# One order for all steps of an attention and channel-mix kernel

## The chip, the core and the metric

The kernel runs on one core of a Trainium2 chip. A core has engines that work side by side, each through its own instructions in their order: TensorE multiplies matrices (PE in the profile; PEld are its weight loads), VectorE (DVE) and ScalarE (ACT) work elementwise, SyncE (SP) issues DMAs and calculates nothing. An instruction that needs another engine's result waits on a semaphore, and everything behind it on its engine waits too. The metric is the time of one execution on the device in microseconds (us); lower is better.

## The reference

Attention inside chunks of 64 tokens for 8 batches of 8 heads, 576 tokens, head size 64; then a channel mix over the 512 joined channels, with 1024 hidden ones. q, k and v are float32, the mu vectors and the weights float64 at the input; the kernel computes with pairs of float32 values, a high part and a low part.

```python
q_c, k_c, v_c = (x.reshape(B, H, nc, 64, D) for x in (q, k, v))
scores = (1 / sqrt(D)) * matmul(q_c, k_c.transpose(0, 1, 2, 4, 3))
attn = softmax(scores)                        # over the last axis
x = matmul(attn, v_c).reshape(B, H, S, D)     # heads joined to 512 channels
x_prev = x shifted by one token, 0 at the start of a batch
xk = mu_k * x + (1 - mu_k) * x_prev
xr = mu_r * x + (1 - mu_r) * x_prev
out = sigmoid(xr @ w_r) * (relu(xk @ w_k) ** 2 @ w_v)
```

## The kernel before

The 4608 tokens are worked in 36 tiles t of 128 tokens (two chunks), or 18 groups g of 256. Every piece of work is a step with a name, a small function that issues a few instructions. An order written out by hand, as a text of step names, says in which sequence the steps issue; since each engine is in order, the text fixes the order on every engine and on every DMA queue. A letter behind a name chooses the engine of an elementwise step (`:A` ScalarE, `:D` VectorE) or, for a load, ScalarE's DMA queue instead of SP's. Before, there are two texts, `START` for the first groups and all weights, and `LATER` for the rest; the second begins where the first has ended. The steps that matter here:

- `nk0 nq0` load q and k of the first three groups in their natural layout, `T` moves them through TensorE (even numbers, 16 matmuls each: T0.6 and T0.4 are the two halves of k, T0.0 and T0.2 of q) and out of PSUM (odd numbers). From the fourth group on, `bq`, `bk` load blocks, each word 4 to 8 DMAs, and `D` transposes them on VectorE (D10.0 for q, D10.1 for k of tile 10). `v` loads v of a tile with four DMAs.
- `S` is the softmax of a tile: scores on TensorE (S.0), maximum, subtraction, exp, sum, scaling. Two tiles of a group share one PSUM tile. `P` transposes the result (P.0), copies it (P.1), multiplies by v (P.2) and writes x (P.3, P.4).
- `s`, `c`, `h` load and convert a weight from float64 bits (`swr1` is half of w_r; c.0, c.1 on ScalarE, c.2, c.3 on VectorE, h.0 high half, h.1 low half). `mu` loads (mu.0), transposes (mu.1, TensorE) and copies the two vectors; `dg` makes diagonal matrices of them.
- `Mk`, `Mr` mix x with its predecessor and split the result in two halves. `R` is the product with w_r and its sigmoid, `K` the product with w_k of a group (24 matmuls of 256 columns) with relu, square and two halves, `V` the product with w_v (steps 0 to 7 of three matmuls of 512 columns, then the multiplication by the sigmoid, then the store).
- From group 4 on, two groups together form the w_k product as a 2 x 2 block product with seven multiplications instead of eight (`U` sums of weights, `Xt` and `X` sums of inputs, `M` the products, `C` and `E` the rest). START with K00 to K13 and the K2, K3 of LATER stand before that; I call the stretch from one to the other the passage, and what follows from V30 on the pairs.
- `W:9` issues nine matmuls on an idle tile (two instructions each) that compute nothing.

Scratch tiles are given out in turn: `bank("k")` alternates between two PSUM banks k0, k1, `bank("o")` between o0 and o1, and `mixed` and `f_relu` go round a few SBUF tiles, in the order of the calls.

```python
    with tc.manual_schedule():
        for word in START.split():
            name, _, e = word.partition(":")
            if name == "W":
                for _ in range(int(e)):
                    nc.tensor.matmul(warm, idle, idle, start=True, stop=True)
            else:
                fn, engine_of = first.pop(name)
                fn(e or engine_of)
```

Of the kernel before, what the change touches and what calls it, by code (L numbers as in the profile page):

```python
# [1261 lines left out]
```

## Time and profile before

| | us |
|---|---|
| median of three runs (608.8 to 612.25) | 609.77 |
| the profiled execution, its own time | 608.68 |
| its span, first to last instruction | 606.9 |
| TensorE busy | 586.3 |
| VectorE busy | 469.8 |
| ScalarE busy | 371.9 |

The span is what the trace shows; 1.8 us of the execution's time lie around it. Busy is the time in which an engine had at least one instruction under way. An engine that waits inside a stretch is not busy; matmuls are pipelined, so a busy TensorE isn't one at its peak.

### The profile page before, as it was taken

To read this page: it belongs to the slowest core of one execution; us is meant where nothing else is said; L and a number is where in the kernel's file an instruction comes from. 1 tells how busy PE (TensorE), PEld (TensorE's weight loads), DVE (VectorE), ACT (ScalarE), POOL (GpSimd) and SP (SyncE) were. 2 spreads that over 40 slices of the span, in tenths; PEclk is the share of its full clock that TensorE was granted. 3 is DMA by queue.
4 is the path that set the end of the run, shared out by engine and by line. 5 is a ranking of instruction groups with operands and counts; after the bars stand their busy time and mean duration, and the time that the engine had idled before them with its cause. 6 is when DMAs were issued, how large, how long until landed. Compare 5 with 4: busy or idle time off the path is not lost.

```text
span 606.9 us, 14236 instructions
## 1 busy us (share of the span) xinstructions
PE 586.3 (97%) x5633; PEld 514.4 (85%) x5633; DVE 469.8 (77%) x991; ACT 371.9 (61%) x599; POOL 0.7 (0%) x6
## 2 busy tenths in 40 slices
PE   6799999997999999999999999999999999999997
PEld 6689888986878987898889888888898889888985
DVE  0788898887999797988796988798869886965321
ACT  3599974372755872689267817791579257924640
POOL 0000000000000000000000000000000000000000
PEclk8899999999999999999999999999999999999999
DMA  9698243244324324434432342334324341000001
GB/s 264 162 312 207 36 112 75 34 91 88 69 43 98 55 55 109 75 68 70 92 65 59 67 95 33 89 66 94 55 63 71 89 80 45 13 36 36 1 18 52
DMA packets 186802, 49.19 MB, mean 81 GB/s; under 512 B 172392, under 2 KB 178544, under 8 KB 186736
## 3 DMA queue, kind: packets, MB, share of 16 engines
q1 hardware_dynamic: 179664, 46.45, 33.7%
q10 hardware_dynamic: 7072, 1.84, 1.3%
q8 instruction: 44, 0.72, 0.5%
q14 instruction: 22, 0.18, 0.1%
HBM read 38.80 MB, written 9.44 MB: 79 GB/s over the span
## 4 chain that ended last, share of the span: by engine, by line
PE 73%; SPq 12%; DMA 6%; DVE 4%; ACT 4%; issue 2%; DVEq 0%; ACTq 0%
PE pv L845 26%; PE m L1143 20%; PE pr L811 13%; SPq L359 9%; PE pk L767 4%; PE s L531 3%; PE xps L611 3%; DMA nat<-in_k 2%; SPq L323 2%; PE pt L588 2%; DMA qT<-in_q 1%; PE trk L484 1%; DMA mus<-in_moe_mu_r 1%; DMA v<-in_v 1%; DMA kT<-in_k 1%
## 5 line engine op out<-in xcount | busy, mean ns | idle before, releaser
L845 PE MATMUL pv<-wv,kk 128*128 128x512 f32 x864 | 209.8, 397 | 0.2 <-ACT sg L827 0.2
L845 PEld LDWEIGHTS pv<-wv,kk 128*128 128x128 f32 x864 | 159.4, 188 | 37.6 <-ACT sg L827 0.6
L811 PE MATMUL pr<-wr,xr 128*128 128x512 f32 x432 | 106.1, 397 | 0.0
L811 PEld LDWEIGHTS pr<-wr,xr 128*128 128x128 f32 x432 | 79.5, 188 | 18.1 <-issue 0.2
L1194 DVE TENSOR_TENSOR kk<-c,kk 128x512 fp32r<-128x512 f32 x56 | 38.0, 684 | 29.1 <-ACT kk L276 29.1
L767 PE MATMUL pk<-xk,wk 128*128 128x256 f32 x384 | 48.0, 283 | 0.9 <-ACT relu L781 0.9
L767 PEld LDWEIGHTS pk<-xk,wk 128*128 128x128 f32 x384 | 46.5, 188 | 1.7 <-ACT relu L781 1.1
L1143 PE MATMUL m<-t,wk 128*128 128x256 f32 x336 | 44.9, 283 | 0.0
L1143 PE MATMUL m<-xk,wk 128*128 128x256 f32 x336 | 43.2, 281 | 0.0
L1143 PEld LDWEIGHTS m<-t,wk 128*128 128x128 f32 x336 | 42.1, 188 | 1.0
L1143 PE MATMUL m<-t,sum 128*128 128x256 f32 x336 | 42.3, 282 | 0.1
L1143 PEld LDWEIGHTS m<-xk,wk 128*128 128x128 f32 x336 | 41.7, 188 | 0.6
L1143 PEld LDWEIGHTS m<-t,sum 128*128 128x128 f32 x336 | 40.7, 188 | 0.6 <-DVE sg L858 0.5
L1162 DVE TENSOR_TENSOR c<-m,c 128x512 f32<-128x512 f32 x42 | 28.6, 686 | 14.2 <-PE m L1143 13.5
L858 DVE TENSOR_TENSOR sg<-pv,sg 128x512 f32<-128x512 f32 x36 | 24.7, 686 | 18.5 <-PE pv L845 18.2
L541 DVE TENSOR_REDUCE m<-s 128x8 f32<-128x512 f32 x36 | 23.7, 683 | 18.3 <-PE s L531 18.3
L276 ACT ACTIVATE x<-xps 128x512 f32<-128x512 f32 (+1 forms) x40 | 20.8, 548 | 26.7 <-DMA qT<-in_q 15.4
L1187 ACT ACTIVATE c<-c 128x512 f32<-128x512 f32 x56 | 35.3, 631 | 1.3
L1181 ACT ACTIVATE c<-c 128x512 f32<-128x512 f32 x42 | 26.3, 626 | 15.8 <-DVE c L1162 15.3
L276 ACT ACTIVATE kk<-c 128x512 fp32r<-128x512 f32 x56 | 34.9, 631 | 1.5
L1031 DVE SCALAR_TENSOR_TENSOR mixr<-d,mu,x 128x128 f32<-128x128 f32 (+1 forms) x124 | 33.3, 333 | 0.2
L531 PE MATMUL s<-kT,qT 64*64 64x64 f32 x1152 | 26.7, 227 | 4.5 <-DVE kT L507 2.3
(108 smaller groups left out, 843.4 us busy)
## 6 DMA issues: line engine op xcount, KB each, us to landing
v<-in_v SPq DMA_DIRECT2D x144, 64.0 KB, 2.6
out<-sg SPq DMA_DIRECT2D x36, 256.0 KB, 2.1
wk_st<-in_moe_w_k SPq DMA_DIRECT2D x4, 1024.0 KB, 6.1
wv_st<-in_moe_w_v SPq DMA_DIRECT2D x4, 1024.0 KB, 14.9
qT<-in_q SPq DMA_DIRECT2D x128, 32.0 KB, 1.9
kT<-in_k SPq DMA_DIRECT2D x128, 32.0 KB, 1.9
qT<-in_q SPq DMA_DIRECT2D x48, 24.0 KB, 1.8
wr_st<-in_moe_w_r ACTq DMA_DIRECT2D x1, 1024.0 KB, 6.4
```

Source lines behind the costliest of these rows:

```text
L276: nc.scalar.activation(to, x, AF.Copy)
L359: queue(e).dma_start(out=to_s[:, i], in_=of[:, i])
L531: nc.tensor.matmul(scores()[halves[e], j, hp, :], qT[halves[j], hp, cols[e]], kT[halves[j], hp, cols[e]], start=True, stop=True,)
L767: nc.tensor.matmul(pk[:, e, :], wk[f // 4][:, a, cb, f % 4 * P : (f % 4 + 1) * P], xk[b][:, cb, :], start=(n == 0), stop=(n == 3 * NB - 1),)
L811: nc.tensor.matmul(pr, xr[a][:, cb, tl * TT : (tl + 1) * TT], wr[b][:, cb, :], start=(n == 0), stop=(n == 3 * NB - 1),)
L845: nc.tensor.matmul(T[f"pv{g}{tl}"], kk[a][:, f, tl * TT : (tl + 1) * TT], wv[b, f // 4][:, f % 4, :], start=(f == 0 and n == 0), stop=(f = ...
L1031: nc.vector.scalar_tensor_tensor(out=to[:, s : s + w], in0=d[:, cb, s : s + w], scalar=mu[:, cb : cb + 1], in1=x[:, cb, c : c + w], op0=AL ...
L1143: nc.tensor.matmul(ps[w][:, e, :], left(n, a, cb, 2 * u + e), right(g, n, b, cb), start=first and i == 0, stop=i == 11, skip_group_check=True,
L1162: nc.vector.tensor_tensor(r(i), ps[where[n]], r(i), ALU.add)
L1181: nc.scalar.activation(r(i), x, AF.Relu)
L1187: nc.scalar.activation(r(i), r(i), AF.Square)
L1194: engine[e].tensor_tensor(lo, r(i), f32(hi), ALU.subtract)
```

## The change

The two texts become one, `ORDER`, over all steps, in another sequence throughout. Each scratch tile is now looked up by name in a table (`HOMES`), which says for the first four groups which bank or tile it takes. The loads of `nq`, `nk` and `v` can choose their queue like the others. Beyond that no step is added or taken away except the fillers: `W:9`, `W:4`, `W:4`, `W:3` become one `W:17` at the head. 92 elementwise steps that ran on ScalarE carry `:D` now. The w_r half `swr1` goes to SP's queue, mu.0 stays on ScalarE's and comes first.

```diff
-START = """
-W:9 Mk2.0:D nk0.0 T0.6 nq0.0 T0.4 swr1.0:A T0.7:A P0.3:D T0.5:A T0.0 T0.2 T0.1:A mu.0 nk1.0
-T0.3:A W:4 S0.0 cwr1.0:A mu.1 S1.0 S0.1:D W:4 T1.4 S0.2:D S0.3:A mu.2:A S1.1:D T1.5:A nq1.0 W:3
-T1.2 S1.2:D S1.3:A S0.4:D S0.5:D S1.4:D T1.0 S1.5:D v0.0 P0.0 cwr1.1:A T1.3:A T1.1:A cwr1.2:D
...
-K01.2:A K01.3:A cwv0.3:D K03.1:A K10.0 cwv1.0:A Mk0.0:D K03.2:A swv3.0 K11.0 bk3.0 bk3.1 bk3.2 bk3.3 S5.1:D
-R11.1:A K01.4:D cwv1.2:D cwv1.3:D bq4.0 bq4.1 bq4.2 bq4.3 hwv0.0:A K10.1:A hwv0.1:D K12.0 V001.0 S4.3:A cwv3.1:A
...
-V10.5 bk4.0 bk4.1 bk4.2 bk4.3 Mr4.2:D V10.6 V10.7 D7.1:D D6.0:D V10.8:D V10.9 V11.6 v7.0 V11.7 Mr5.2:D V11.8:D V11.9
-LATER = """
...
-bk5.2 V21.0 Mk7.1:D P9.1:A V21.1 Mr6.1:A Mk6.3:D V21.2 Mk7.2:A bk5.3 V21.3 Mk7.3:D D10.0:D V21.4
-D11.0:D V21.5 Mr6.2:D U61.0:A V21.6 V20.8:D V21.7 Mr7.0:D V20.9 K30.0 Mr7.1:A D10.1:D D11.1:D
...
+ORDER = """
+W:17
+mu.0:A nk0.0 P0.3:D nq0.0 swr1.0 nk1.0 nq1.0 T0.6 T0.4 T0.7:A v0.0 T0.0 T0.5:A T0.2 T0.1:D T0.3:A
+S0.0 nk2.0 S1.0 cwr1.0:A mu.1 S0.1:D swr0.0 cwr1.1:A S1.1:D S0.2:D T1.6 mu.2:A cwr1.2:D T1.4 v1.0
+S0.3:A S1.2:D T1.7:A S0.4:D T1.5:A T1.0 S0.5:D S1.3:A T1.1:A S1.4:D P0.0 T1.2 dg.0:A P0.1:D S1.5:D
+nq2.0 cwr1.3:D P1.0 T2.6 swk1.0 P1.1:D P0.2 T1.3:A hwr1.0:D P0.4:A S2.0 hwr1.1:D v2.0 S3.0
...
+V001.3 S5.3:A hwv3.1:D K11.3:A V001.4 S4.5:D bk4.0 K11.4:D V001.5 S5.4:D S5.5:D V001.6 K10.3:D
+K10.4:D P4.0 D7.0:D K12.1:A bq4.3 V001.7 D7.1:D P4.1:A D6.1:D K12.2:A P5.0 V001.10:D K12.3:A P4.2
+P5.1:A K12.4:D V11.0 P4.4:A V001.8:D K13.0 Mk4.0:D v6.0 Mk4.1:D Mr4.0:D V10.0 Mk4.2:A V10.1
+K13.1:A V001.9 V11.1 K13.2:A P5.3:D V001.11 Mk4.3:D K13.3:A V11.2 bq4.1 D6.0:D Mr4.1:A V10.2
...
+V20.5 V21.7 bk5.2 Mk6.3:D Mk7.2:A V20.6 Mk7.3:D V20.7 Mr7.0:D v9.0 K31.0 Mr6.2:D Mr7.1:A D10.0:D
+D11.0:D V21.8:D K30.0 V11.9 K31.1:A D10.1:D v10.0 K31.2:A D11.1:D Mr7.2:D U61.0:A V20.8:D K31.3:A
+P8.3:D S10.0 P9.3:D K30.1:A U61.1:D P9.2 U51.1:D K30.2:A V10.9 S11.0 P9.4:D K30.3:A v11.0 R30.0
...
+V170.2 V171.3 V171.4 V171.5 V171.6 V170.3 V170.4 V170.5 V170.6 V170.7 V171.7 V170.8:D V171.8:D
+V170.9 V171.9
...
     def bank(tag, shape, name):
-        tag = turn(("k0", "k1")) if tag == "k" else turn(("o0", "o1")) if tag == "o" else tag
+        if tag in ("k", "o"):
+            tag = PLACE[name]
         return ps_m.tile(shape, F32, tag=tag, name=name)
...
-                    nc.sync.dma_start(
+                    queue(e).dma_start(
                         out=dst[s // 2 : (s + n) // 2, :, :, :],
...
-        for word in LATER.split():
+        for word in ORDER.split():
             name, _, e = word.partition(":")
```

The old order ended in `V171.6 V171.7 V171.8:D V171.9`, with V170 stored before.

## Rows read from the trace of the kernel before

**Rows 1.** Busy time on the page: us, share of the span, instructions.

```profile
PE 586.3 (97%) x5633; PEld 514.4 (85%) x5633; DVE 469.8 (77%) x991; ACT 371.9 (61%) x599; POOL 0.7 (0%) x6
```

**Rows 2.** Busy time by stretch: stretch (us), its length, then busy time and instructions of PE, PEld, DVE, ACT, POOL, the granted TensorE clock as a share of 2.4 GHz, the DMA engines' busy share, GB/s.

```profile
21.08:45.00 23.92, 21.56 (x365) 18.88 (x366) 21.31 (x36) 22.47 (x45) 0.00 (x0) 1.00 0.70 238
108.00:170.00 62.00, 57.31 (x646) 50.48 (x645) 51.94 (x110) 35.32 (x56) 0.00 (x0) 1.00 0.34 70
170.00:512.00 342.00, 339.36 (x3341) 298.01 (x3345) 289.97 (x646) 215.70 (x352) 0.00 (x0) 1.00 0.35 71
...
19.26:58.60 39.34, 36.98 (x495) 32.67 (x495) 35.02 (x49) 35.86 (x62) 0.00 (x0) 0.98 0.76 230
58.60:108.40 49.80, 49.80 (x418) 43.44 (x417) 44.37 (x87) 36.23 (x53) 0.00 (x0) 1.00 0.33 73
```

**Rows 3.** What TensorE waited for: waiting line, released by, us in total, times, longest.

```profile
PE trk L484 <- DMA nat<-in_k: 3.2, 1, 3.2
PE mu_t L374 <- DMA mus<-in_moe_mu_r: 3.1, 1, 3.1
PE s L531 <- DVE kT L507: 2.3, 1, 2.3
```

**Rows 4.** The start in order of time: start, length (us), engine, line, operation, out<-in, shape, count.

```profile
1.05 3.67 PE L914 MATMUL warm<-idle 128*128 128x128 f32 x18 [1.05 <-DVE x L628]
...
7.89 3.38 PE L484 MATMUL trk<-ident,nat 128*64 128x128 f32 x32 [3.17 <-DMA nat<-in_k]
...
11.09 2.00 PE L484 MATMUL trq<-ident,nat 128*64 128x128 f32 x32
...
13.03 1.16 PE L914 MATMUL warm<-idle 128*128 128x128 f32 x8
...
14.12 0.69 PE L531 MATMUL s<-kT,qT 64*64 64x64 f32 x32
...
17.90 0.24 PE L374 MATMUL mu_t<-ident,mus 8*128 8x8 f32 x1 [3.08 <-DMA mus<-in_moe_mu_r]
...
18.07 1.13 PE L531 MATMUL s<-kT,qT 64*64 64x64 f32 x32
...
19.26 0.69 DVE L541 TENSOR_REDUCE m<-s 128x8 f32<-128x512 f32 x1 [18.25 <-PE s L531]
```

**Rows 5.** Busy time by stretch, columns as in rows 2, for the first loads (the last column is GB/s): SP's queue alone, then with w_r on ScalarE's, then SP's alone again.

```profile
2.00:3.00 1.00, 1.00 (x7) 1.00 (x6) 0.00 (x0) 0.54 (x1) 0.00 (x0) 1.00 0.49 132
3.00:6.00 3.00, 1.72 (x11) 1.53 (x10) 0.00 (x0) 0.00 (x0) 0.00 (x0) 1.00 1.04 395
6.00:12.00 6.00, 4.11 (x48) 4.04 (x48) 0.00 (x0) 1.27 (x2) 0.00 (x0) 0.72 1.19 297
```

**Rows 6.** Busy time by stretch, columns as in rows 2, cut where the granted clock changes.

```profile
1.05:4.01 2.96, 2.96 (x14) 2.96 (x15) 0.00 (x0) 1.28 (x1) 0.25 (x1) 1.00 0.55 185
4.01:7.42 3.41, 0.71 (x6) 0.52 (x5) 0.00 (x0) 0.00 (x0) 0.00 (x0) 1.00 1.05 362
7.42:10.84 3.42, 2.95 (x28) 2.98 (x30) 0.00 (x0) 0.63 (x1) 0.00 (x0) 0.50 1.22 291
...
17.66:21.08 3.42, 3.18 (x41) 2.90 (x41) 1.78 (x3) 0.36 (x1) 0.00 (x0) 0.50 0.90 151
```

**Rows 7.** SP's queue in order of time from 60 to 156 us, columns as in rows 4; the first and the last of eleven groups of issues that follow one another without a pause, and three between.

```profile
74.59 10.18 SPq L359 DMA_DIRECT2D nat<-in_k  x16
...
101.36 0.85 SPq L862 DMA_DIRECT2D out<-sg  x2
102.31 2.61 SPq L323 DMA_DIRECT2D v<-in_v  x4
104.96 16.56 SPq L359 DMA_DIRECT2D nat<-in_k  x32
...
140.87 8.00 SPq L359 DMA_DIRECT2D nat<-in_k  x16
148.97 6.51 SPq L862 DMA_DIRECT2D out<-sg  x2
```

**Rows 8.** TensorE in order of time, columns as in rows 4, in the passage (P8.0, K30.0, S10.0) and behind it (S16.0, P16.0).

```profile
139.18 1.17 PE L588 MATMUL pt<-ident,p 128*128 128x128 f32 x8 [1.36 <-DVE p L561]
...
145.78 3.00 PE L767 MATMUL pk<-xk,wk 128*128 128x256 f32 x24
...
152.14 1.20 PE L531 MATMUL s<-kT,qT 64*64 64x64 f32 x64 [2.27 <-DVE kT L507]
...
240.85 1.69 PE L531 MATMUL s<-kT,qT 64*64 64x64 f32 x64 [1.33 <-issue]
...
257.85 1.17 PE L588 MATMUL pt<-ident,p 128*128 128x128 f32 x8 [0.35 <-DVE p L561]
```

**Rows 9.** Groups of VectorE's instructions by line and shape: count, busy us, mean ns of one, idle before.

```profile
L1194 DVE TENSOR_TENSOR kk<-c,kk 128x512 fp32r<-128x512 f32 x56 | 38.0, 684 | 29.1 <-ACT kk L276 29.1
...
L278 DVE CAST wr<-wr_st 128x1024 fp32r<-128x1024 f32 x1 | 0.7, 694 | 0.0
```

**Rows 10.** The end in order of time, columns as in rows 4.

```profile
599.64 3.65 PE L845 MATMUL pv<-wv,kk 128*128 128x512 f32 x15
...
603.33 0.69 DVE L858 TENSOR_TENSOR sg<-pv,sg 128x512 f32<-128x512 f32 x1 [4.90 <-PE pv L845]
604.05 0.33 SPq L862 DMA_DIRECT2D out<-sg  x1
```

More of the change, by code (lines that the diff above doesn't have):

```diff
@@ new lines @@
+V41.5 P14.4:A Mk13.0:D V50.0 bk8.3 Mr13.0:D V50.1 V41.6 V41.7 Mk13.1:D bq8.3 Mr13.1:A V50.2 V50.3
+V41.8:D Mk13.2:A V50.4 bq8.1 P15.3:D Mr13.2:D P15.4:A V50.5 D17.1:D V50.6 D16.1:D V51.0 V40.9
+Mk13.3:D V41.9 R60.0 Mk14.0:D v16.0 Mr14.0:D Mk14.1:D V50.7 R60.1:A D16.0:D R61.0 v17.0 V50.8:D
+D17.0:D Mk15.0:D Mk15.1:D V51.1 R61.1:A V50.9 Xt37.0:D Mr14.1:A S16.0 S17.0 X7t3.0:A Mr14.2:D
+V51.2 bq9.0 S16.1:D V51.3 S16.2:D V51.4 S17.1:D S16.3:A V51.5 bk9.0 S16.4:D R70.0 S16.5:D S17.2:D
+bq9.1 X7t3.1:D S17.3:A S17.4:D P16.0 M6a.0 bq9.3 S17.5:D R70.1:A Xt17.0:D M6a.1 C6a.0:A Xt17.1:D
@@ new lines @@
+V170.2 V171.3 V171.4 V171.5 V171.6 V170.3 V170.4 V170.5 V170.6 V170.7 V171.7 V170.8:D V171.8:D
+V170.9 V171.9
+"""
+HOMES = dict(
+    F0="""
+relu_0_0 relu_0_2 relu_1_0 relu_1_2 relu_2_0 relu_2_2 relu_3_0 relu_3_2
+""",
+    F1="""
+relu_0_1 relu_0_3 relu_1_1 relu_1_3 relu_2_1 relu_2_3 relu_3_1 relu_3_3
+""",
+    X0="""
+diag_k0 d_3 mixk_4 mixr_5 d_7
+""",
+    X1="""
+diag_k1 mixk_3 mixr_4 d_6 mixk_7
+""",
+    X4="""
+diag_r0 mixr_3 d_5 mixk_6 mixr_7
+""",
+    X5="""
+diag_r1 d_4 mixk_5 mixr_6
@@ new lines @@
+""",
+    k0="""
+trk1_0 trq0_0 mu_t trk0_1 trq1_1 trk0_2 trq1_2 pk_0_1 pk_0_3 pk_1_1 pk_1_3 pk_2_1 pk_2_3 pk_3_1
+pk_3_3
+""",
+    k1="""
+trk0_0 trq1_0 trk1_1 trq0_1 trk1_2 trq0_2 pk_0_0 pk_0_2 pk_1_0 pk_1_2 pk_2_0 pk_2_2 pk_3_0
+pk_3_2
+""",
+    o0="""
+warm mxr_0 mxr_1 pr_0_1 mxk_2 pr_1_1 pv_0_1 pv_1_1 pr_2_1 pv_2_1 pr_3_1 pv_3_1
+""",
+    o1="""
+mxk_0 mxk_1 pr_0_0 mxr_2 pr_1_0 pv_0_0 pv_1_0 pr_2_0 pv_2_0 pr_3_0 pv_3_0
+""",
+)
+PLACE = {name: tag for tag, names in HOMES.items() for name in names.split()}
@@ L649, in mixed @@
     def mixed(shape, name):
-        return mx.tile(shape, F32, tag=turn(("X0", "X1", "X4", "X5")), name=name)
+        return mx.tile(shape, F32, tag=PLACE[name], name=name)
     ON_PE = (0, 1, 2)
@@ L776, in f_relu @@
         def f_relu(e):
-            r = T[f"r{g}{fp}"] = full(turn(("F0", "F1")), [P, 2, G], f"relu_{g}_{fp}")
+            r = T[f"r{g}{fp}"] = full(PLACE[f"relu_{g}_{fp}"], [P, 2, G], f"relu_{g}_{fp}")
             if e == "D":
@@ L907, in tile_chunk_attention_channel_mix @@
     moe_v(1, (1,))
-    first = do.take()
-    with tc.manual_schedule():
-        for word in START.split():
-            name, _, e = word.partition(":")
-            if name == "W":
-                for _ in range(int(e)):
-                    nc.tensor.matmul(warm, idle, idle, start=True, stop=True)
-            else:
-                fn, engine_of = first.pop(name)
-                fn(e or engine_of)
-    assert not first
     sums = {}
@@ L1226, in tile_chunk_attention_channel_mix @@
             differences(g)
-    later = do.take()
+    steps = do.take()
     with tc.manual_schedule():
-        for word in LATER.split():
+        for word in ORDER.split():
             name, _, e = word.partition(":")
-            fn, engine_of = later.pop(name)
-            fn(e or engine_of)
-    assert not later, list(later)
+            if name == "W":
+                for _ in range(int(e)):
+                    nc.tensor.matmul(warm, idle, idle, start=True, stop=True)
+            else:
+                fn, engine_of = steps.pop(name)
+                fn(e or engine_of)
+    assert not steps, list(steps)
 _INS = ["q", "k", "v", "moe_mu_k", "moe_mu_r", "moe_w_k", "moe_w_v", "moe_w_r"]
```

303 lines of the change are left out of this document (144 added, 159 removed).

## Prediction

> **What bounds the kernel now.** I read the page first, then stretches, then waits, then the order of time where waits stand. The page gives TensorE 586.3 us of a 606.9 us span [rows 1]: 20.6 us are left at most to whoever fills its pauses, and TensorE's work itself isn't changed. The stretches [rows 2] say where they are. From 58.6 to 108.4 us TensorE is busy throughout, and from 170 to 512 us for 339.36 of 342 us. The pauses stand in the start, in 108 to 170 us (57.31 of 62 us) and at the very end. The start holds more than its pauses: its fillers, matmuls on an idle tile that compute nothing, are counted as busy too, 18 of them before the first transpose and 8 more at 13 us [rows 4].
>
> The waits of TensorE [rows 3] name them: 3.2 us for the first k, 3.1 us for mu, 2.3 us for VectorE's transposed k. Those are symptoms. The start in order of time [rows 4] shows the cause: VectorE's first score step (S0.1) begins at 19.26 us, though the scores it reads were computed from 14.12 us on. TensorE stood at `mu.1` until 17.90 us and ran S1.0 behind it at 18.07 us; the reduction waited for S1.0, which shares its tile. From 21.08 to 45 us VectorE is busy 21.31 and ScalarE 22.47 of 23.92 us [rows 2]: once started, these two set the pace until the weights are converted, so a later start of VectorE delays everything behind it.
>
> **The change, part by part.** *The start.* Removed: the 1 MB of w_r on ScalarE's queue beside the first k and q; two groups of fillers between the steps (8 matmuls each) and one of 6; mu's place behind `swr1.0`. Moved: mu to the front of ScalarE's queue, w_r to SP behind nq0, mu.1 behind S1.0. Walked with the rows: alone on its queue the first k (0.5 MB) moves at 132 GB/s or more; with w_r beside it the two queues move 395 GB/s, most of it w_r, and k and q behind it 297 GB/s [rows 5]. Starting near 2 us, k lands between 2.0 + 1.8 + 1 = 4.8 us and 2.0 + 4.0 + 1 = 7.0 us, against 7.76 to 7.89 us now [rows 4]. The 34 fillers of `W:17` end near 6.9 us (14 in the first 2.96 us [rows 6], 20 at 1.16 us for eight [rows 4]), so T0.6 starts at about 6.9 us either way. It now runs at 1.2 GHz, 32 transposing matmuls in 3.38 us; at full clock 32 take 2.00 us [rows 4], so the second half of k ends near 8.9 us. q's two halves wait for one eviction each (0.6 us) and end near 10.9, the last eviction near 11.8, S0.0 and S1.0 (0.69 and 0.5 more) near 13.1. VectorE starts S0.1 at about 13.2 instead of 19.26 us: -6.1 us. `T0.1` on VectorE (0.69 us) lies before that.
>
> From there to `K02.0`, a channel-mix product that both orders reach behind the same conversions, I count VectorE's steps ahead of it in both orders: 18 of 1024 columns that convert weights, at twice a 512-column step (22 us), and the rest, softmax steps and low halves of x at about 0.60 us (a 0.68 us step [rows 9] overlaps the next), give 37.8 us before and 39.5 us after; TensorE's work there is 37.1 against 40.6 us, because the new order has one K step more ahead. Before, K02.0 began 39.3 us after VectorE's start with VectorE busy for 35.02 us of it [rows 2]. With the same pauses the 6.1 us survive. The fillers between steps are gone, so I give back 0.5 us for clock: with the least (0 us) and the most (3.4 us, half-clock work of the size of the second cold stretch [rows 6], 3.18 us of 3.42, all on the path). Term: -5.6 us; bounds -8 (VectorE's 4.3 us of pauses halved) and -2.5 us (k no earlier than now, only the 3.1 us mu wait gone).
>
> *The passage.* SP is one queue in order and never pauses from 74.6 to 149 us [rows 7]: 32 issues take 16.56 us, 16 take 8.00 us. Behind the two stores of V001 at 101.36 us stand, before, v6, all 32 issues of bk4, v7, the 16 of bq5, v8 and v9, the 16 of bk5 and two more stores: at 2.6 us a v load, 0.5 us a block issue and 0.5 us a store, 2.6 + 16.6 + 2.6 + 8.0 + 5.2 + 8.0 + 1.0 = 44 us; by the rows they end at 149 us, 47.6 us behind the stores; TensorE's work in the order from there to D10.1 is 31 V steps of 0.73 [rows 10], five K of 3.0 [rows 8], two R of four V steps' size and the small products, 48.5 us. With the landing that is even, and S10.0 waited 2.27 us for `kT` [rows 8]. After: bk4.0, bk4.1 and bq4.3 (24 issues) stand ahead of the stores; behind them 40 issues of the fifth block, v7, v8 and the 32 of the sixth, 20.7 + 2.6 + 2.6 + 16.5 = 42.4 us, 46 with the 3.6 us by which the rows ran over, against 28 V, six K, two R and small products, 50.5 us. SP has some 4 us to spare, so the 2.3 us go. Late next is VectorE: P8.0's 1.36 us came from it [rows 8], and TensorE comes some 6 us earlier to a VectorE that has the same work (44.37 of 49.80 us from 58.6 to 108.4 us [rows 2]). I take -2.5 of the 4.7 us of pauses in this stretch; bounds -4.7 and +2 us (a pause like P8.0's at one pair more than now).
>
> *Engines.* 92 steps go from ScalarE to VectorE, 86 of them from V30 on: 48 copies, 14 relus, 14 squares, the rest from PSUM. What ScalarE gives up is hidden, since it is busy 215.70 of 342 us [rows 2]. VectorE's price has no row for a 512-column copy: its 1024-column CAST takes 0.69 us, half of that 0.35 us is the lower bound; the upper is the 0.684 us of a two-operand step [rows 9]. A copy is nearest the CAST, so 0.35 for 48 + 14, 0.6 for the other 30: 40 us. In 170 to 512 us VectorE goes from 289.97 to about 323 us of 342 us, 94%: hidden, but with little over. With the upper bound it would be 339 us.
>
> *Where the new order is thin.* I list, for each matmul step behind V30, what it reads and how much TensorE work the order puts between. Before, 5 places have less than one V step, after 30, half of them D steps ahead of scores and softmax ahead of transposes. Before, the pairs S16/S17 and P16/P17 were such places and cost 1.33 and 0.35 us [rows 8]. Thirty places make some 15 pairs; at 0.35 us each 5 us, at 0.84 us (the mean) 12.6 us. The low price is right where VectorE keeps up. I take 5 us, less the 2.5 us of waits that stand there now: +2.5 us; bounds -2.5 and +10 us.
>
> *End.* Now V171.8 (0.69 us) and one store follow the last matmul at 603.3 us [rows 10]. After, V170.8 lies on VectorE under the last V step, and two 256 KB stores go out within a microsecond: +0.3 us, between 0 and 0.7.
>
> The turns of table loads for exp and sigmoid are 34 in both orders, no term.
>
> *Sum:* -5.6 - 2.5 + 2.5 + 0.3 = -5.3 us on the profiled execution's 608.68 us, which is 1.1 us under the median of the runs shown, 609.77 us: 603.4 us. I say 603.0, a little of the 1.1 us and of the start's better bound set against each other.
>
> *A rule against it.* TensorE is granted half clock from 7.42 to 10.84 us, after 0.71 us of work in 3.41 us, and from 17.66 to 21.08 us, after it had stood for mu [rows 4, 6]. The Trainium skill (TensorE: Matmul & The Clock Gate, "HAM oscillation — how this bites in real kernels") says that an engine which idles between bursts starts the next one cold; the trace agrees with both stretches. By that rule the pauses behind T1.4, which `W:4` and `W:3` fill now, turn cold in the new order. That is a rival below.
>
> **The rivals.** A measurement of this kernel tells about 0.5% from no change: under 606.7 us is faster, over 612.8 us slower.
>
> *Everything fits as listed:* -8 - 4.7 - 2.0 + 0.3: 594.3 us. For it: the two orders give VectorE a steady share, and the thin places are an order's own pace. Against it: two engines near 95% never met without pauses in this trace (VectorE 89% from 19 to 58 us [rows 2]).
>
> *The thin places cost their mean:* -5.6 - 2.5 + 10 + 0.3: 610.9 us, no change. For it: S16's 1.33 us. Against it: they stand in a stretch where TensorE lost only 2.6 us.
>
> *The start stays cold or short:* half clock at the rule's place costs 3.4 us, or k lands no earlier: -2.5 - 2.5 + 2.5 + 0.3: 606.5 us. For it: TensorE has only about 5 us of work between 13 and 20 us. Against it: VectorE paces that stretch, not TensorE.
>
> *VectorE becomes the bound (slower):* if the moved copies cost 0.68 us, VectorE needs 339 us in the stretch of 342. At the 95% it could hold, that is 357 us, +15 us: 608.7 - 8.1 + 15 + 0.3 = 616 us. It decides from about 0.6 us for a copy. Against it: the CAST row.
>
> **How the numbers follow.** Forecast 0.52 (its own range 598 to 606.5 us), everything fits 0.14, thin places 0.14, cold or short start 0.11, VectorE the bound 0.09. The range 595 to 611 us leaves out the last and the tails of the first two. Faster: 0.50 of the forecast, 0.14, and 0.06 of the short start: 0.70. Same: 0.02 + 0.11 + 0.05 + 0.01: 0.19. Slower: 0.08 of the bound and 0.03 of the thin places: 0.11.
>
> **What would show it.** Right: VectorE's first score reduction near 13 us; K02 near 52 to 53 us; no wait of scores for `kT` behind a k load near 145 us; VectorE busy some 510 us, a 512-column copy on it near 0.35 us; TensorE's waits from 170 us on near 5 us in 15 small pieces. Wrong: S0.1 later than 16 us, SP without a pause up to D10.1 again, copies at 0.6 us, or TensorE waits over 10 us behind V30.

## Result and the profile after

The new kernel takes 593.55 us (median of 4 runs, 592.10 to 594.96) where the old one beside it takes 609.28 us (608.45 to 612.25): a ratio of 0.9733 (95% interval 0.9691 to 0.9776). The forecast was 603.0 us, with a range of 595 to 611: the direction was right, the gain was more than twice the forecast, and the time lies 1.4 us below the range. The profiled execution took 594.24 us, of which 592.5 us are the span.

The page's busy line, to be read against [rows 1]:

```profile
PE 582.0 (98%) x5627; PEld 508.9 (86%) x5627; DVE 514.6 (87%) x1083; ACT 322.4 (54%) x507; POOL 0.7 (0%) x6
```

TensorE is busy 4.3 us less (one half-clock stretch in the start instead of two is in that); the other 10 us of the gain are pauses. The stretches, columns as in [rows 2], the first cut at VectorE's first score reduction:

```profile
12.41:21.08 8.67, 6.38 (x72) 5.13 (x72) 8.49 (x15) 7.62 (x22) 0.00 (x0) 0.83 1.19 256
21.08:45.00 23.92, 22.57 (x333) 20.09 (x333) 21.43 (x33) 20.93 (x32) 0.00 (x0) 0.99 0.92 280
...
108.00:170.00 62.00, 62.00 (x657) 54.10 (x656) 58.84 (x132) 40.77 (x64) 0.00 (x0) 1.00 0.36 70
170.00:512.00 342.00, 340.57 (x3334) 297.98 (x3333) 315.73 (x693) 182.48 (x288) 0.00 (x0) 1.00 0.35 72
```

From 108 to 170 us TensorE has no pause left (busy 57.31 of 62 us before). In 170 to 512 us VectorE went from 289.97 to 315.73 us, 92%, and TensorE gained 1.2 us all the same. What TensorE waited for, against [rows 3]; the first number is the sum in us:

```profile
PE mxr L729 <- issue: 1.4, 1, 1.4
PE pt L617 <- DVE p L590: 1.2, 1, 1.2
PE trq L513 <- ACT kT L305: 1.1, 1, 1.1
...
PE m L1159 <- ACT sg L856: 0.5, 1, 0.5
PE pv L874 <- DVE c L1178: 0.5, 1, 0.5
PE pr L840 <- ACT sg L856: 0.3, 1, 0.3
```

The first three stand before 27 us, the others far behind 170 us; no wait of TensorE for k, mu or the transposed k is left. The start in order of time, against [rows 4]:

```profile
1.05 5.68 PE L1249 MATMUL warm<-idle 128*128 128x128 f32 x34 [1.05 <-DVE x L657]
...
6.66 1.97 PE L513 MATMUL trk<-ident,nat 128*64 128x128 f32 x32
...
11.19 1.16 PE L560 MATMUL s<-kT,qT 64*64 64x64 f32 x64 [0.72 <-ACT qT L305]
...
12.28 0.22 PE L403 MATMUL mu_t<-ident,mus 8*128 8x8 f32 x1
...
12.41 0.69 DVE L570 TENSOR_REDUCE m<-s 128x8 f32<-128x512 f32 x1 [2.08 <-PE s L560]
```

**Where the time came from.** The two orders reach a step of one name with different work behind them, so I compare TensorE's *lag*: the time at which a step starts, less the sum of fixed lengths of all TensorE steps ahead of it in its own order. The lengths come from steps that stand back to back in the trace (K 2.93, R 2.80, diagonal mix 1.85, M 1.42, T 0.95, V 0.70, S 0.55, value product of attention 0.50, transposed p 0.43 us, fillers 0). Lag in us, by work done; behind 170 some 8 to 9 us of growth in the kernels before and after are no waits, but steps a little longer than their fixed length:

```
work done (us)            2    10    20    60   142   170   250   400   563
before                  9.2  17.6  19.2  21.6  27.5  28.3  32.4  36.3  38.8
after                   6.6  11.9  13.6  13.8  14.3  15.1  17.0  20.9  24.2
old_s1_ahead_of_mu      8.5  16.9  18.4  20.8  27.0  27.7  32.1  34.9  37.3
old_with_new_loads      6.0   9.9  12.2  13.9  20.7  21.3  30.2  34.0  36.4
start_new_rest_old      6.4  11.7  13.7  13.9  19.1  19.7  23.4  26.5  28.9
new_steps_back_on_...   6.8  11.1  13.8  13.9  14.5  15.4  17.9  27.0  30.4
old_rest_with_moves     7.1  11.5  12.7  13.0  19.5  20.1  23.7  29.4  35.9
new_again               7.6  11.9  12.9  13.1  13.7  14.5  15.7  19.4  22.9
new_softmax_first2      6.3   9.1  10.9  11.0  11.6  12.4  13.6  17.9  21.3
```

Of the 14.4 us between the two spans, 7.8 us are there at 60 us of work (start), 5.4 us come between 60 and 170 (before grows by 6.7 us, after by 1.3: the passage), 1.4 us behind that (10.5 against 9.1 us), and the end gives 0.1 us back.

### The profile page after: what moved, and what is told of

Same layout as the page of the kernel before. It is cut to its first block, busy times and chain, and to the rows that moved or that the text cites. A ratio compares the mean times of both kernels' runs of the same rounds, so it can differ in the third digit from the quotient of the medians.

```text
span 592.5 us, 14233 instructions
## 1 busy us (share of the span) xinstructions
PE 582.0 (98%) x5627; PEld 508.9 (86%) x5627; DVE 514.6 (87%) x1083; ACT 322.4 (54%) x507; POOL 0.7 (0%) x6
## 4 chain that ended last, share of the span: by engine, by line
PE 83%; DVE 8%; SPq 3%; DMA 2%; issue 1%; ACT 1%; ACTq 0%; DVEq 0%
PE pv L874 28%; PE m L1159 21%; PE pr L840 14%; PE pk L796 8%; PE s L560 3%; PE xps L640 3%; PE pt L617 2%; SPq L388 1%; PE mxr L729 1%; PE trq L513 1%; PE warm L1249 1%; PE mxk L729 1%; DVE sg L887 1%; SPq L352 1%; DVE mixr L1047 1%
## 5 line engine op out<-in xcount | busy, mean ns | idle before, releaser
L874 PE MATMUL pv<-wv,kk 128*128 128x512 f32 x864 | 218.9, 399 | 0.6 <-DVE c L1178 0.5
L874 PEld LDWEIGHTS pv<-wv,kk 128*128 128x128 f32 x864 | 157.1, 188 | 35.5 <-DVE c L1178 0.7
L1159 PE MATMUL m<-t,sum 128*128 128x256 f32 x336 | 43.9, 282 | 0.0
L1159 PEld LDWEIGHTS m<-t,sum 128*128 128x128 f32 x336 | 42.0, 189 | 1.0
L856 ACT ACTIVATE sg<-pr 128x512 f32<-128x512 f32 x36 | 21.5, 598 | 38.4 <-PE pr L840 31.8
L305 ACT ACTIVATE x<-xps 128x512 f32<-128x512 f32 (+1 forms) x36 | 19.0, 547 | 35.4 <-DMA kT<-in_k 11.9
L305 ACT ACTIVATE c<-m 128x512 f32<-128x512 f32 x42 | 25.0, 596 | 24.0 <-PE m L1159 17.7
L1197 ACT ACTIVATE c<-c 128x512 f32<-128x512 f32 x31 | 19.5, 630 | 22.7 <-DVE c L1178 22.6
L1203 ACT ACTIVATE c<-c 128x512 f32<-128x512 f32 x42 | 26.5, 630 | 9.7 <-DVE c L1195 9.0
L305 ACT ACTIVATE kk<-c 128x512 fp32r<-128x512 f32 x40 | 25.3, 632 | 11.5 <-DVE c L1201 10.5
```

What stands on the lines that cost most here:

```text
L305: nc.scalar.activation(to, x, AF.Copy)
L856: nc.scalar.activation(sg, T[f"pr{g}{tl}"], AF.Sigmoid)
L874: nc.tensor.matmul(T[f"pv{g}{tl}"], kk[a][:, f, tl * TT : (tl + 1) * TT], wv[b, f // 4][:, f % 4, :], start=(f == 0 and n == 0), stop=(f = ...
L1159: nc.tensor.matmul(ps[w][:, e, :], left(n, a, cb, 2 * u + e), right(g, n, b, cb), start=first and i == 0, stop=i == 11, skip_group_check=True,
L1197: nc.scalar.activation(r(i), x, AF.Relu)
L1203: nc.scalar.activation(r(i), r(i), AF.Square)
```

## Experiments

**Stage by stage.** Three kernels join the orders: one order up to a step, then the other with what remains.

```diff
 start_new_rest_old:    ORDER(new) up to V001.0 + ORDER(old), steps done left out
 new_upto_v30_rest_old: ORDER(new) up to V30.0  + ORDER(old), steps done left out
 old_upto_v30_rest_new: ORDER(old) up to V30.0  + ORDER(new), steps done left out
```

> The new order up to V001.0 (the first step of the paired value product), then the old order with the steps that remain. Read from the two traces, TensorE's lag behind its own nominal work is 21.6 us before and 13.8 us after at that place, so by the theory that the gain adds up stage by stage this kernel is 7.5 us faster than before: about 602 us (ratio 0.988). The prediction's term for the start was 5.6 us: 604 us. Rival: a passage that begins earlier also loses its waits, because the loads of k and q get ahead; then 597 us or less. By the stage theory the waits of scores for the transposed k (2.3 us) and of P8 (1.4 us) stand as before, since their load queue is measured from the stores of V001, which come earlier by the same amount.

598.12 us, ratio 0.9824 (0.9801 to 0.9847): 10.2 us from the new start alone, more than either theory gave it. The lag at 60 us is that of the new kernel (13.9 us); 2 us more come behind it, where the old waits of P8.0 (1.36 us) and K33 (0.90 us) are gone. Why these two go with an earlier start was not tested; K33's is back (0.90 us) in start_and_k4_early. The one that stays is the wait for the transposed k:

```profile
PE s L556 <- DVE kT L532: 3.1, 1, 3.1
```

It grew from 2.27 to 3.09 us, and TensorE came out of it at half clock; the next rows are the wait and what follows it, columns as in [rows 2]:

```profile
140.60:143.70 3.10, 0.01 (x2) 0.03 (x1) 0.85 (x2) 0.00 (x0) 0.00 (x0) 1.00 0.35 103
144.00:147.41 3.41, 3.41 (x68) 3.29 (x61) 2.15 (x7) 3.16 (x6) 0.00 (x0) 0.50 0.02 5
```

The old kernel's stretch behind its shorter wait stayed at full clock:

```profile
152.14:155.50 3.36, 3.36 (x83) 3.29 (x83) 2.10 (x6) 2.81 (x6) 0.00 (x0) 1.00 0.02 5
```

> The new order up to V30.0, then the old order with the steps that remain: the new start and the new passage without the new steady stretch. By the stage theory start and passage together give 7.5 + 5.2 us: 596.5 us, the passage being the difference to the kernel with only the new start. By the prediction's terms they give 8.1 us: 601 us. Rival: the passage lost its waits only because later steps were rearranged and taken off ScalarE; then it is no better than the kernel with only the new start, 602 us.

605.49 us, 0.9963 (0.9941 to 0.9984). Its lag is 13.4 us at 60 and 14.0 at 142 us of work, so the passage is as free of waits as in the new kernel with the later steps still in their old places: the rival falls. The total says nothing, because the joint itself makes TensorE wait:

```profile
PE m L1155 <- ACT sg L852: 8.2, 1, 8.2
```

> The old order up to V30.0, then the new order with the steps that remain: 86 of the 92 steps moved to VectorE, the thin places and the new end are in it, the new start and passage are not. The prediction's terms for this stretch were +2.5 us (thin places) and +0.3 us (end): 612 us. By the two traces, whose lag grows by 11.3 us behind V30 before and by 9.9 us after, it is 1.4 us faster than before: 608 us. If the thin places cost their mean it is 617 us, if VectorE binds more.

617.65 us, 1.0152 (1.0125 to 1.0178). Inconclusive for the same reason: between 142 and 170 us of work the joint costs 9.5 us of lag, in three waits of 1.9 to 4.1 us (V31.0, M4a.1, S12.0) that neither kernel has. Behind 170 its lag grows by 8.0 us, less than the old kernel's 10.5, with the thin places in it.

**The start.** Four kernels change one thing each.

```diff
 old_s1_ahead_of_mu (old order)
-S0.0 cwr1.0:A mu.1 S1.0 S0.1:D
+S0.0 cwr1.0:A S1.0 mu.1 S0.1:D
 old_with_new_loads (old order)
-W:9 Mk2.0:D nk0.0 T0.6 nq0.0 T0.4 swr1.0:A ... mu.0 nk1.0
+W:9 Mk2.0:D mu.0:A nk0.0 T0.6 nq0.0 swr1.0 T0.4 ... nk1.0
 new_w12 (new order)
-W:17
+W:12
 new_wr_beside (new order)
-nq0.0 swr1.0 nk1.0
+nq0.0 swr1.0:A nk1.0
```

> The old kernel with one swap: S1.0 ahead of mu.1 on TensorE. Everything else, the loads too, as before. The prediction's reading: VectorE's first score step is held by S1.0, so S0.1 starts near 15.5 instead of 19.26 us and the kernel gains 3 us or more: 605 us. The other reading: what counts in the start is TensorE's own lost time; it still stands at mu.1 until 17.9 us, so it gains at most 1 us: 607.5 us or no measurable change.

606.77 us, 0.9976 (0.9951 to 1.0001), no difference that can be told. VectorE's first reduction came 4.0 us earlier (15.28 us), but TensorE stood at `mu.1` all the same (2.42 us, until 17.63 us), and the lag at 60 fell by 0.8 us only. An earlier start of VectorE alone, with TensorE still held at `mu.1`, buys next to nothing.

> The old kernel with the new order of the first loads alone: mu first on ScalarE's queue, w_r on SyncE's queue behind the first k and q; the order on the engines, fillers included, as before. k lands at 5.1 us as in the new kernel and mu is there long before it is wanted. If the loads carry the start, S0.1 comes at about 12 us and the kernel takes 598 to 599 us, like the kernel with the whole new start (598.1 us). If the new order of engine steps in the start (fillers ahead, mu behind S1.0) matters too, it stays 2 us or more above that.

603.07 us, 0.9916 (0.9886 to 0.9946), with runs from 599.3 to 606.8. The lag at 60 us is 13.9: the order on two queues alone gives all of the new start's 7.7 us. TensorE waits neither for the first k nor for mu there, and has no half-clock stretch in the start; VectorE's first reduction comes at 12.38 us. Its time is worse than that of start_new_rest_old because two later waits for k are longer here (S10.0 3.56 us, S16.0 3.78 us in the profiled run, 606.29 us) and each comes with 6.83 us at half clock, in these rows at S16.0:

```profile
235.61:239.00 3.39, 2.69 (x65) 2.56 (x66) 3.35 (x10) 0.00 (x0) 0.00 (x0) 0.50 0.59 170
239.00:242.44 3.44, 3.44 (x9) 2.64 (x8) 3.37 (x11) 0.36 (x1) 0.00 (x0) 0.50 0.46 96
```

So the loads carry the start, but not to the end by themselves.

> The new kernel with 24 fillers in front instead of 34. In its trace k lands at 5.06 us, but TensorE runs fillers until 6.7 us. With 24 they end near 5.4 us, T0.6 begins 1.2 us earlier, q (landed at 6.7 us) is there for T0.0, and the kernel takes 592.3 us if TensorE's work alone sets the pace. Rival: between 12 and 25 us TensorE waits for evictions and diagonal matrices whatever happens earlier, then no change (593.5 us). Rival: with fewer fillers a stretch falls to half clock, then up to 1 us slower than that.

593.23 us, 0.9757 (0.9729 to 0.9786): no change. T0.6 starts at 6.47 instead of 6.66 us, although there are ten fillers fewer. In this run they follow one another every 0.21 us up to 6.1 us; in the new kernel's run that pace doubles at 4.4 us. The granted clock reads 1.00 in both, but it says nothing here: the traces' first record of the clock stands at 6.79 us in new_w12 and at 4.46 us in the new kernel, and time ahead of it counts as 1.00. The count behind TensorE's busy time is that of its instructions in each microsecond of new_w12:

```profile
4.00:5.00 1.00, 1.00 (x6) 1.00 (x6) 0.00 (x0) 0.00 (x0) 0.00 (x0) 1.00 1.19 313
5.00:6.00 1.00, 1.00 (x7) 1.00 (x6) 0.00 (x0) 0.00 (x0) 0.00 (x0) 1.00 1.22 307
6.00:7.00 1.00, 1.00 (x11) 0.78 (x12) 0.00 (x0) 0.00 (x0) 0.00 (x0) 1.00 1.03 359
```

> The new kernel with the 1 MB of w_r back on ScalarE's queue (behind mu), beside the first k and q. If sharing the DMA engines with w_r is what held k, k lands near 7.8 us again, T0.6 starts 1.1 us later than now and q's two halves later still, so the kernel loses 1 to 2 us: 595 us. If k would have landed early anyway (mu off the queue being what counts), no change: 593.5 us.

593.10 us, 0.9750 (0.9726 to 0.9774): no change. k landed at 5.23 us with w_r on the other queue, issued 0.9 us behind it; in the old kernel both were issued at 0.73 us and k landed at 7.76. Only q came later (9.38 instead of 6.70 us), just in time for T0.0 at 9.57 us; in this run the fillers lasted until 7.7 us. w_r need not leave ScalarE's queue if it is issued behind mu.

**The passage.** Two kernels on top of start_new_rest_old.

```diff
 start_and_k4_early
-V001.8:D V001.9 V11.0 ... v6.0 Mr5.1:A ... V10.5 bk4.0 bk4.1 bk4.2 bk4.3
+V001.8:D bk4.0 bk4.1 bk4.2 bk4.3 V001.9 V11.0 ... v6.0 Mr5.1:A ... V10.5
 start_k4_early_k8_two_queues: the same, and
-bk8.2 bk8.3
+bk8.2:A bk8.3:A
```

> The kernel with the new order up to V001.0 and the old order behind it (598.1 us), with one more edit: the 32 issues of the fifth block of k (bk4) ahead of the two stores of V001 on SyncE's queue instead of behind v6. If the load queue makes S10.0 wait (3.09 us there, and TensorE at half clock for 3.4 us behind it), the wait goes and the kernel gains 3 to 5 us: 593.5 to 595 us. Rival: VectorE is late next, a wait at P8 or P10 takes the place of most of it, 597 us. Rival: the stores, now behind 16 us of issues, hold the sigmoid's buffers and TensorE waits there, 598 us or more.

596.72 us, 0.9819 (0.9769 to 0.9869): 1.4 us under start_new_rest_old by the medians, inside the intervals, not the 3 to 5 us. The half-clock stretch is gone, 2.06 us of the wait are not. SyncE's queue in this kernel shows why:

```profile
75.83 16.08 SPq L384 DMA_DIRECT2D nat<-in_q  x32
91.96 16.24 SPq L384 DMA_DIRECT2D nat<-in_k  x32
108.29 0.85 SPq L887 DMA_DIRECT2D out<-sg  x2
...
125.98 5.25 SPq L348 DMA_DIRECT2D v<-in_v  x8
131.28 8.00 SPq L384 DMA_DIRECT2D nat<-in_k  x16
```

The queue has no pause to be filled, so moving a load forward moves others back; the issues of the k that S10.0 needs end at 139.3 us, 1.0 us earlier than in start_new_rest_old, and the wait is 1.0 us shorter. The new kernel's queue has v9 (four issues) behind that k and ends it 3.2 us earlier, and 2.4 us more of TensorE's work stands ahead of S10.0 there. The new kernel's queue:

```profile
126.07 8.00 SPq L388 DMA_DIRECT2D nat<-in_q  x16
134.12 1.93 SPq L388 DMA_DIRECT2D nat<-in_k  x4
136.14 3.50 SPq L352 DMA_DIRECT2D v<-in_v  x4
```

> As start_and_k4_early, with two of the four parts of the ninth block of k (bk8.2, bk8.3) issued by ScalarE instead of SyncE. In the old kernel the transposes of this block stand idle 2.98 us for its load, and S16.0 behind them makes TensorE wait 1.33 us. If that wait too is SyncE's issue time (8 issues of 0.49 us less), it goes: 0.9 to 2 us under start_and_k4_early, 592 to 593 us. If it is the price of a thin place (too little TensorE work between transposes and scores), it stays, no change.

595.78 us, 0.9796 (0.9755 to 0.9837), not the 592 to 593 us; the 0.9 us between the two are less than either interval. The trace is plainer than the time: S16.0's wait (0.91 us in start_and_k4_early) is gone, and VectorE stood 1.62 instead of 2.56 us for this k. In the old kernel it is the same, on VectorE:

```profile
240.03 1.30 DVE L507 STREAM_TRANSPOSE kT<-kT 128x512 f32<-128x512 f32 x2 [2.98 <-DMA kT<-in_k]
```

and on SyncE's queue, the 32 issues ahead of it:

```profile
222.68 7.74 SPq L359 DMA_DIRECT2D qT<-in_q  x16
230.51 7.79 SPq L359 DMA_DIRECT2D kT<-in_k  x16
```

**The steps moved to VectorE.**

```diff
 new_steps_back_on_scalar (new order, 86 steps behind V30.0), for instance
-E100.0:D Mr10.1:D X9t1.0:D P14.1:D
+E100.0:A Mr10.1:A X9t1.0:A P14.1:A
 new_x_back: 30 of them (high halves and copies of x)   new_e_back: 44 (relu squares)
 old_rest_with_moves: start_and_k4_early with all 86 on D, in the old order
 new_dose1: 40 more E*.2 on D   new_dose2: those and 24 more Mk/Mr high halves
```

> The new kernel with the 86 steps behind V30 that it moved from ScalarE to VectorE put back on ScalarE, the order unchanged. Theory one: the move is neutral, both engines have room there, TensorE never waits for either, and the time stays within 1.5 us of the new kernel (593.5 us). Theory two: the thin places are harmless only because of the move (the short chains run on the engine that is free), then ScalarE, whose work in 170 to 512 us rises from 182 to about 230 us, makes TensorE wait and the kernel is 5 us or more slower. Theory three, the one behind the prediction: VectorE at 92% costs something, and with the steps back the kernel is 2 us or more faster.

602.95 us, 0.9905 (0.9876 to 0.9935): 9.4 us slower than the new kernel. ScalarE is busy 210.07 of the 342 us, less than the old kernel's 215.70, so its busy time alone doesn't explain the loss. In the profiled run (600.38 us) TensorE's waits behind 170 us sum to 6.2 us. The longest (2.21 us, at M12a.0) is for the sigmoid at the end of this piece of ScalarE's queue, which a copy of x held up:

```profile
423.91 0.63 ACT L302 ACTIVATE t<-rawt 128x512 fp32r<-128x512 f32 x1 [1.79 <-DVE rawt L1099]
424.56 1.28 ACT L853 ACT_TABLE_LOAD   x1
425.86 0.60 ACT L853 ACTIVATE sg<-pr 128x512 f32<-128x512 f32 x1
```

The second (1.86 us, at M10a.4) begins elsewhere. A copy stands behind eight load issues on ScalarE, which its busy time leaves out; VectorE waits for the copy, and TensorE for a multiplication behind it on VectorE. ScalarE's queue, then VectorE:

```profile
355.73 3.71 ACTq L385 DMA_DIRECT2D qT<-in_q  x8
359.49 0.63 ACT L302 ACTIVATE t<-rawb 128x512 fp32r<-128x512 f32 x1 [3.13 <-DMA qT<-in_q]
...
360.16 0.69 DVE L1112 TENSOR_TENSOR t<-rawb,t 128x512 fp32r<-128x512 f32 x1 [1.81 <-ACT t L302]
```

> The new kernel with 30 of the 86 steps back on ScalarE: the high halves and copies of x and of its differences, which wait for VectorE's products. All 86 back cost 9.4 us, and there the sigmoid R120.1 stood in ScalarE's queue behind such a copy that itself stood 1.79 us for VectorE. If that is the mechanism, these 30 carry most of the loss: 597 to 601 us. If ScalarE's load counts, they carry their share of its time, 30/86 of 9.4: 596.8 us.

598.17 us, 0.9853 (0.9816 to 0.9890): 4.6 us slower than the new kernel, with the same waits at M12a.0 (2.04 us) and M10a.4 (1.35 us). By itself this time doesn't rule out the share by load, 596.8 us; the next run does.

> The new kernel with the 44 steps of the relu squares (relu, square, rounded copy) back on ScalarE. If the handover from VectorE to ScalarE is what costs, these cost little, since their inputs come from ScalarE itself or from PSUM: 593.5 to 595 us. If ScalarE's load counts, 44/86 of 9.4 us: 598.3 us.

595.11 us, 0.9785 (0.9758 to 0.9813): 1.6 us slower, within the intervals no change. By load the 44 would have cost more than the 30; by the medians they cost a third, and neither wait is there. What costs at these two waits is the place of the copies of x in ScalarE's in-order queue: ahead of a sigmoid at one, behind load issues at the other. The two sum to 6.2 of 9.4 us; what the remaining 12 copies from PSUM cost, or the three groups together, was not separated.

> start_and_k4_early (596.7 us: new order up to V001.0, old order behind it, bk4 early) with the 86 steps that the change moves put on VectorE, in the old order. If the move helps by itself (shorter chains, ScalarE's queue free for sigmoid and exp), 594 us or less, and the new order behind V001 is worth nothing beyond its moves and loads. If the move only pays in the new order, which spreads VectorE's steps, VectorE at about 94% comes late here and it is 597 us or more.

603.51 us, 0.9941 (0.9914 to 0.9968): with the moves the old order is 6.8 us slower than start_and_k4_early. In the profiled runs 1.8 us of the difference stand ahead of the first moved step, at S10.0 (a wait of 3.42 us there, 2.06 in start_and_k4_early). Behind 142 us of work its lag grows 16.4 us, that of start_and_k4_early 10.1: 6.3 us that the moves cost. TensorE waits for VectorE's copies there, though VectorE is busy 309.54 of 342 us, less than in the new kernel:

```profile
PE xps L636 <- DVE pT L303: 2.6, 4, 1.0
...
PE pv L870 <- DVE kk L1206: 1.3, 3, 0.7
```

The assignment to engines and the order belong together: the new order without the moves loses 9.4 us, the old order with them some 6 us.

> The new kernel with 40 more rounding copies of relu squares (512 columns each, ScalarE) put on VectorE, order unchanged. In the new kernel's trace such a copy takes VectorE 0.418 us: 16.7 us more, VectorE busy in 170 to 512 us from 315.7 to 332 of 342 us (97%). If VectorE is not yet the bound, 593.5 us within 1.5 us; if it begins to bind at 95%, as one rival of the prediction had it, 332/0.95 - 342 = 8 us slower: 601 us.

595.33 us, 0.9785 (0.9748 to 0.9822), 1.8 us over the new kernel by the medians, which the intervals don't tell from nothing. VectorE is busy 323.31 of 342 us (95%), not the 332 expected: only 26 of the 40 more instructions fall in the stretch, so 97% was not tried.

> The new kernel with 64 more copies put on VectorE (the 40 of new_dose1 and 24 high halves of x): 26.8 us more, VectorE wants 342.5 of the 342 us between 170 and 512 us. If VectorE can be packed nearly full, 3 to 5 us slower than the new kernel (597 to 599 us); if 95% is what it can hold, 18 us slower: 612 us.

598.48 us, 0.9831 (0.9796 to 0.9867), 5 us over the new kernel; VectorE 328.67 of 342 us (96%), again less than planned. In this order it can be filled to 94 or 95% with next to no loss, and the step to 96% costs. Whether it is the fullness that costs, or the place of these 24 copies in VectorE's queue, was not separated.

**Does lag saved in the start reach the end?**

```diff
 new_softmax_first (new order, W:12), steps of the start
-cwr1.1:A S1.1:D S0.2:D T1.6 mu.2:A cwr1.2:D T1.4 v1.0 S0.3:A S1.2:D T1.7:A S0.4:D T1.5:A T1.0 S0.5:D S1.3:A
-T1.1:A S1.4:D P0.0 T1.2 dg.0:A P0.1:D S1.5:D nq2.0 cwr1.3:D P1.0 T2.6 swk1.0 P1.1:D P0.2 T1.3:A
+cwr1.1:A S0.2:D S1.1:D T1.6 mu.2:A T1.4 v1.0 T1.7:A S0.3:A S1.2:D S0.4:D T1.5:A S1.3:A T1.0 S0.5:D T1.1:A
+S1.4:D T1.2 T1.3:A P0.0 P0.1:D S1.5:D dg.0:A cwr1.2:D nq2.0 P0.2 cwr1.3:D P1.0 T2.6 swk1.0 P1.1:D
 new_softmax_first2: also cwr1.3 behind P1.1      new_again: the new kernel unchanged
```

> The new kernel with 24 fillers (no change by itself, 593.2 us) and 14 steps of the start in another order: the first softmax (S0.2, S0.3, S0.4) and the eviction of the second k ahead of weight conversion steps and of the diagonal matrices. In the trace TensorE stands 1.09 us for that eviction at T1.0, 1.18 us for the softmax at P0.0 and 0.51 us at P1.0. If TensorE's lag in the start carries through to the end, as the start kernels show, 1.5 to 2.5 us faster: 591 us. Rival: the conversions, now later, make TensorE wait at the first R or K step near 40 us, and it is no faster than 593.2 us.

591.05 us, 0.9737 (0.9714 to 0.9760), 2.2 us under new_w12.

> new_softmax_first (591.05 us) with one more step moved: the copy P1.1 on VectorE ahead of the conversion step cwr1.3. In new_softmax_first the scores S2.0 stand 1.38 us for P1.1, which frees their bank, and P1.1 comes 1.22 us later because of that step. If lag saved in the start carries through, about 1 us less: 590 us, some 3.5 us under the new kernel run beside it. If the wait moves to the conversion (the first R step near 41 us), 591 us.

591.11 us (590.12 to 591.34), 0.9737 (0.9702 to 0.9773).

> The new kernel as it is, beside new_softmax_first2 on the same chip: 593.5 us. It tells how far two measurements of one kernel lie apart; both theories expect no difference from the first measurement beyond 1 us.

593.39 us (592.16 to 594.69), 0.9780 (0.9743 to 0.9817). On one chip all five runs of new_softmax_first2 lie below all six of the new kernel; 2.3 us by the medians, with 2.1 us less lag at 60 and 1.6 us less at the end. TensorE from 12 to 21 us in new_again:

```profile
12.00:21.00 9.00, 6.08 (x133) 4.99 (x133) 7.44 (x15) 7.95 (x20) 0.00 (x0) 1.00 1.20 254
```

and in new_softmax_first2:

```profile
12.00:21.00 9.00, 7.45 (x146) 6.08 (x142) 8.60 (x16) 8.48 (x24) 0.00 (x0) 1.00 1.20 251
```

This version beats the kernels before and after. Its last edit bought nothing over new_softmax_first: S2.0's wait went, others took its place.

## Why the prediction was right or wrong

**The start (-5.6 us; measured -7.8 us of lag, -10.2 us with what follows from it).** Right: T0.6 at 6.9 us (6.66; 6.46 to 7.94 in the other kernels with this start), S0.1 at 13.2 (12.41), k landing in 4.8 to 7.0 us (5.06). Wrong was the step from there to the term. It took VectorE's start as the clock of the whole start and a step of the same name, K02.0, as the mark of progress. K02.0 came at 54.37 us, 4.2 us earlier, which looks short of the forecast; but 40.6 us of TensorE's work lie ahead of it in the new order and 37.1 in the old, numbers that the prediction itself gives, and with these 3.5 us the gain is 7.7. old_s1_ahead_of_mu refutes the cause: 4.0 us for VectorE bought 0.8 us. What the prediction called symptoms, TensorE's waits for k and mu (3.17 and 3.08 us) and the two half-clock stretches beside them, was the loss: the loads alone take them away, and the 7.7 us with them (old_with_new_loads). The cause named for the late k, w_r beside it, was half right: issued at the same moment as k it goes with a k at 7.76 us, issued 0.9 us behind with one at 5.23 (new_wr_beside).

**The rule against it.** The granted clock was 0.50 from 18.11 to 21.52 us, behind three pauses of 0.7, 1.1 and 1.2 us, where the fillers had been taken out. The Trainium skill (TensorE: Matmul & The Clock Gate, "HAM oscillation — how this bites in real kernels") has an engine that idles between bursts start the next one cold; this trace agrees with the place, but of twelve kernels with this start and these pauses only this one and start_new_rest_old have such a stretch. The price was small: the lag at 60 is 13.8 and 13.9 us in these two, 13.0 to 13.9 in the other ten. The prediction's +0.5 us lies within that, the rival's 3.4 us doesn't. It was also too high a bound: 3.4 us at half clock delay TensorE's work by at most half of that, and behind S10.0 in start_new_rest_old such a stretch cost 1.7 us (lag 4.8 us, the wait 3.09).

**The passage (-2.5; measured -5.4).** The sum over SyncE's queue was right in kind: the 2.3 us went, and with the old passage S10.0 starts 3.1 to 3.4 us after the last issue of its k, wherever that falls (before, start_new_rest_old, start_and_k4_early). The queue has still no pause over 1 us from 67 to 136 us, which the prediction listed as a sign of being wrong; what changed is that this last issue ends 6.7 us ahead of S10.0 (142.79 us). The Trainium skill (Perfetto Trace Analysis, "What 'DMA-bound' means") names this bound, an issuing engine whose track is solid with DMA slices; the rows of that queue agree. Two sizes were off. The wait was held back against P8.0 and a VectorE that would be late next, bound +2; it was not, neither here nor in start_new_rest_old. And a wait costs more than its length when a half-clock stretch follows. That the new order only had to move k loads forward was refuted by start_and_k4_early; fewer issues ahead of the needed k, and more work on TensorE ahead of its use, are what the new kernel has instead. Neither was tested by itself.

**The thin places (+2.5; measured -1.4 for all behind 170 us of work).** This is the step that failed, 3.9 of the some 9 us by which the sum was off. Its price came from S16.0 and P16.0 [rows 8], read as what a thin place costs and taken for some fifteen pairs. S16.0 stood for a load: VectorE's transposes had themselves waited 2.98 us for k, and the wait went when half of that load changed its queue. P16.0's 0.35 us stayed (0.35 or 0.36 us in every kernel with the old order there, also without S16.0's wait), so it was a price, but of one place. In the new kernel, with 30 thin places by the prediction's count, all of TensorE's waits behind 100 us sum to 1.4 us, in four small pieces. That holds for its assignment of steps: in the same order with the 86 steps back on ScalarE they sum to 6.2 us. Why they cost so little there was not shown.

**The engines (0 for the moves; 9.4 us in the new order).** "What ScalarE gives up is hidden" failed, as new_steps_back_on_scalar shows: hidden by busy share, which leaves out ScalarE's load issues, but not by place in the queue. The prices of the moved steps were near: a copy between SBUF tiles took 0.418 us (0.35), a copy from PSUM and a square 0.684 to 0.686 (0.6), VectorE in all 514.6 us (510):

```profile
L307 DVE COPY pT<-pt 128x512 f32<-128x512 f32 x11 | 7.3, 684 | 0.5 <-PE pt L617 0.5
L307 DVE CAST kk<-c 128x512 fp32r<-128x512 f32 x16 | 6.6, 418 | 1.2 <-ACT c L1203 1.1
```

**The rivals.** "Everything fits as listed" (594.3 us, chance 0.14) is what happened, to 0.1 us of the profiled time, the argument against it (two engines near 95% never met without pauses) being the one that failed. Its hit is partly luck: the -8 us for the start was VectorE's pauses halved, and the -7.8 us came from TensorE's waits. The range, which began at 595 us, left this rival's own time out. VectorE as the bound was rightly small: at 323 us in the stretch, where the prediction saw the new kernel, no cost can be told from none, at 329 us 5 us. The 95% that VectorE "could hold" came from no row; new_dose2 ran at 96%. **The end** took 0.1 us more, not 0.3.

## What to carry to other kernels

Measure progress by the work done, not by a step's name, when an order changes. Before a wait is priced as the cost of a tight place, follow the instruction that ended it one step further back; here it ended at an in-order load queue. An engine's busy share doesn't tell whether a step on it is free: what stands behind it in the queue, what it waits for and which load issues stand ahead of it, does, so an order and its assignment to engines are to be tested together.

## What the hardware showed that was not expected

TensorE's longer waits often came with a stretch at a granted clock of 0.50, but their length alone didn't decide it. At S10.0 and S16.0 the waits of 2.76 (old_s1_ahead_of_mu) and 3.09 us had one of 3.41 us, those of 3.42, 3.56 and 3.78 us one of 6.83 us; those of 2.06, 2.27 and 2.83 us (old_upto_v30_rest_new) had none. With the wait of 3.09 us the lag grew 4.8 us.

At the very start TensorE ran fillers at 0.21 us each and later at 0.11 us. The change came between 4.0 and 7.2 us, and in each trace that shows it within one filler of the first record of the clock, which is 1.00. For the time ahead of it there is no record, so the 1.00 in the column (in the first stretch of [rows 6] too) is not a measured clock; the pace is nearly half. The moment differed between runs, which moved S0.1 by 1.5 us among kernels with the same start, but the lag at 60 us of work only between 13.0 and 13.9 us.
